# An attention and mixer block on one core: a modulation vector in the prologue, a rebuilt start of the tail, regrouped mixer channels, and hints on all final branches

## The chip, the core and the metric

The kernel runs on one core of one Trainium2 chip. The metric is the device time of one execution in microseconds (us), and each kernel was run several times. "Span" is the part of that time which the profiler's trace covers; 4 to 6 us of each execution lie outside it. Five engines matter here: TensorE (PE in the profile, its weight loads PEld), VectorE (DVE), ScalarE (ACT), GpSimd (POOL) and SyncE (SP), which in this kernel does nothing but issue DMA transfers.

## The reference, cut to what matters

```python
mod = (silu(c) @ w_mod).reshape(1, 6, 1, 640)       # sa, ca, ga, sb, cb, gb: vectors 0 to 5
h = layernorm(x) * (1 + ca) + sa                    # x: 2048 x 640
x = x + ga * attention(h, k_cache, v_cache, wq, wo) # 32 heads of 128, 2048 keys
h = layernorm(x) * (1 + cb) + sb
x = x + gb * B(h)

def B(x):                                           # the mixer and an MLP
    h = gelu(layernorm(x) @ w1)                     # 640 channels in 4 groups of 160
    hs = concat(shift(h[group], by +1, -1, +2, -2 rows)) @ w2
    x1 = x + hs
    return x1 + gelu(layernorm(x1) @ w3) @ w4       # 1728 wide
```

## The kernel before: the parts that the change and the argument touch

The kernel records every operation with a planned duration and a priority, and a scheduler written in Python sets the order of each engine before the program is built. The 2048 queries are four chunks of 512 (`NC`), and the 32 heads are eight groups of four. A *step* is one head on one chunk. It has eight score pairs of two 128x512 matmuls each, and one exponential of 128x1024 per pair. So there are 128 steps and 1024 exponentials.

```python
MS = 17
for n, p in enumerate((2, 4, 3, 5)):            # four modulation vectors, in steps 17 to 24
    dma("SP", ... w_half[n % 2], w_mod[:, p * D:(p + 1) * D] ...)                 # 800 KB each
    for hf in range(2):
        for k in range(KT):                     # five 128x320 matmuls per half
            P.op("PE", ... matmul(m, s_bc[:, k, :], w_half[n % 2][:, k, sl]) ...)

def load_head(h):                               # heads 1 to 4 in the prologue, the others later
    load_k(h, pr, need=from_slot(n))            # four DMA transposes
    load_v(h, pr + 1, need=from_slot(n + 1))    # 512 KB

# ... cut: ln1, q_proj, step, wo_group ...
def mlp_in(ch, prio):                           # the mixer's input: two layernorms of one chunk
    tail = ch == NC - 1
    eng = "DVE" if tail else "POOL"             # chunks 0 to 2: GpSimd; ACT for the roots
    # ... cut ...

TAIL = ("A0 WO B0 B1 B2 A1 B3 A2 ...").split()  # A: mixer in, WO: last projection, B: mixer out, C, D: MLP
# ... cut ...
for (p0, p1, dl) in segs[n]:                    # 128 channels cross a group's edge: 9 GELUs per chunk
    P.op("ACT", ... activation(us_ap[p0:p1, n, ch * QC + 2 + dl: ...], m[p0:p1, :], GELU) ...)

# ... cut: the last instruction on each engine jumps over a general fallback
br = eng.br_cmp(redo[e], 0, comp_op="IS_EQ", on_true="done", on_false="general")
if eng is nc.tensor:
    br.branch_hint(hint["PE"])
```

## Time and profile before

| | before |
|---|---|
| time, median of 3 | 1400.83 us (1400.35 to 1401.30) |
| span of the profiled run | 1394.5 us |
| PE busy | 1367.3 us, 98% |
| first score matmul of the attention | 16.54 us |
| end of the last exponential | 1204.95 us |
| from there to the end of the span | 189.5 us |

Next, the stretches of the kernel before in which the change works: busy us of each engine (with counts), the mean granted PE clock, the busy share of the DMA engines and GB/s.

```profile
core 0: us, PE busy (x) PEld busy (x) DVE busy (x) ACT busy (x) POOL busy (x), PEclk, DMA share, GB/s
...
40.00:50.00 10.00, 9.89 (x108) 7.13 (x109) 4.20 (x11) 9.44 (x11) 0.00 (x0) 1.00 0.69 189
...
1200.00:1210.00 10.00, 9.54 (x86) 6.03 (x86) 6.63 (x19) 8.88 (x14) 7.96 (x9) 1.00 0.59 186
1210.00:1220.00 10.00, 6.32 (x31) 3.43 (x30) 3.43 (x8) 8.33 (x12) 4.77 (x4) 0.83 0.53 94
1220.00:1230.00 10.00, 9.13 (x56) 5.36 (x56) 9.51 (x25) 6.27 (x11) 1.74 (x2) 1.00 0.18 35
```

PE has a hole in 1210 to 1220, where the clock is also below 1: the clock record has it at half from 1215.66 on, for 3.41 us. These are its waits in the tail (who waited for whom, us in total, times, longest), and ScalarE's table loads there:

```profile
PE f_S L668 <- ACT f_PQ L836: 3.3, 1, 3.3
PE f_S L850 <- ACT f_PQ L836: 0.8, 1, 0.8
PE f_S L832 <- ACT f_PQ L836: 0.8, 1, 0.8
```

```profile
L836 ACT ACT_TABLE_LOAD x3 | 3.8, 1283 | 1.1 <-POOL f_PQ L825 1.1
...
L477 ACT ACT_TABLE_LOAD x2 | 2.6, 1283 | 0.0
L478 ACT ACT_TABLE_LOAD x2 | 2.6, 1283 | 0.0
```

L836 is the mixer's GELU, L477 and L478 the logarithm and exponential for the reciprocal roots. PE waits for ScalarE, and ScalarE spends 9 us of some 20 on seven table loads. A load costs its own 1.28 us and little more here: one starts at 1207.92 us, as the GELU before it ends, and the next operation starts at 1209.22, 1.30 us later.

### The profile page before, as it was taken

What the parts mean: (1) busy time and instruction counts of PE and PEld (TensorE: products, weight loads), DVE (VectorE), ACT (ScalarE), POOL (GpSimd) and SP (SyncE); (2) the same over time, 40 slices, a digit from 0 to 9 for tenths busy, and PEclk for the clock granted to TensorE, in tenths of its full rate; (3) what the DMA queues carried; (4) which work ended last, traced back from release to release, by engine and by line L of the source; (5) the groups of instructions that cost most, each with busy time, mean ns of one, the idle gap of its engine ahead of it and who ended that gap; (6) DMA issues with size and microseconds to landing.
All of it is one profiled execution on the core that took longest, in us unless ns stands there. A gap on an engine that the chain in (4) does not pass through costs nothing.

```text
span 1394.5 us, 29726 instructions
## 1 busy us (share of the span) xinstructions
PE 1367.3 (98%) x12941; PEld 943.8 (68%) x13176; DVE 518.6 (37%) x1337; ACT 1125.9 (81%) x1195; POOL 123.8 (9%) x106
## 2 busy tenths in 40 slices
PE   8999999999999999999999999999999999899998
PEld 6667776776777777777776777777777666555554
DVE  5453323233323332233323332333223345585552
ACT  5988888888888889888888888888988888864222
POOL 0000000000000000000000000001233376600000
PEclk9999999999999999999999999999999999999999
DMA  9652623261215221241115112612353112411210
GB/s 204 128 107 38 136 57 86 49 107 35 47 35 88 54 47 35 58 84 39 43 24 99 32 39 31 107 35 47 54 107 98 17 36 51 111 39 48 34 39 24
DMA packets 258963, 88.82 MB, mean 64 GB/s; under 512 B 236625, under 2 KB 257554, under 8 KB 258834
## 3 DMA queue, kind: packets, MB, share of 16 engines
q1 hardware_dynamic: 256210, 85.41, 30.9%
q8 instruction: 104, 1.70, 0.5%
q10 hardware_dynamic: 2624, 1.51, 0.5%
q14 instruction: 25, 0.20, 0.1%
HBM read 43.48 MB, written 2.62 MB: 33 GB/s over the span
## 4 chain that ended last, share of the span: by engine, by line
PE 96%; ACT 2%; issue 1%; DVE 0%; DMA 0%; POOL 0%; ACTq 0%; POOLq 0%
PE f_O L731 34%; PE f_S L712 29%; PE f_M L643 10%; PE f_M L668 10%; PE f_S L890 2%; PE f_M L890 2%; PE f_S L877 2%; PE f_O L877 2%; ACT f_PQ L714 1%; PE f_S L850 1%; PE f_M L850 1%; PE f_S L413 1%; PE f_S L832 1%; ACT f_PQ L836 1%; PE f_O L832 0%
## 5 line engine op out<-in xcount | busy, mean ns | idle before, releaser
L714 ACT ACTIVATE f_PQ<-f_S 128x1024 bf16<-128x1024 f32 x1024 | 1041.5, 1024 | 143.5 <-PE f_S L712 106.4
L731 PEld LDWEIGHTS f_O<-f_KV,f_PQ 128*128 128x128 bf16 x8192 | 593.7, 98 | 231.9 <-ACT f_PQ L714 0.5
L731 PE MATMUL f_O<-f_KV,f_PQ 128*128 128x129 bf16 x8192 | 720.2, 220 | 7.8 <-ACT f_PQ L714 0.3
L712 PE MATMUL f_S<-f_PQ,f_KV 128*128 128x512 bf16 x1856 | 671.3, 379 | 5.3 <-ACT f_PQ L714 2.2
L676 DVE TENSOR_TENSOR f_y<-f_M,f_y 128x320 f32<-128x320 f32 x192 | 94.4, 492 | 524.1 <-PE f_M L668 524.1
L668 PE MATMUL f_M<-f_wo,f_OO 128*128 128x320 bf16 x992 | 270.2, 299 | 0.0
L712 PEld LDWEIGHTS f_S<-f_PQ,f_KV 128*128 128x128 bf16 x2048 | 196.2, 97 | 34.4 <-ACT f_PQ L714 3.9
L643 PE MATMUL f_M<-f_hT,f_wq 128*128 128x512 bf16 x608 | 170.8, 379 | 2.2 <-DVE f_hT L557 0.5
L511 POOL TENSOR_TENSOR f_y<-f_y,f_mod 128x640 f32<-128x640 f32 x40 | 61.4, 1542 | 1056.9 <-DVE f_y L676 1049.5
L668 PEld LDWEIGHTS f_M<-f_wo,f_OO 128*128 128x128 bf16 x992 | 95.1, 98 | 27.9
L740 DVE TENSOR_TENSOR f_OO<-f_O,f_rl 128x256 bf16<-128x256 f32 x256 | 108.4, 423 | 8.3
L646 DVE CAST f_PQ<-f_M 128x512 bf16<-128x512 f32 x128 | 88.5, 691 | 54.3 <-PE f_M L643 53.7
L643 PEld LDWEIGHTS f_M<-f_hT,f_wq 128*128 128x128 bf16 x640 | 62.3, 98 | 62.9 <-DVE f_hT L557 1.0
L738 DVE RECIPROCAL f_rl<-f_O 128x2 f32<-128x2 f32 x256 | 43.5, 170 | 47.2 <-PE f_O L731 42.9
L880 ACT ACTIVATE f_OO<-f_O 128x512 bf16<-128x512 f32 (+1 forms) x28 | 16.7, 596 | 36.2 <-PE f_O L877 36.1
L674 DVE COPY f_y<-f_M 128x320 f32<-128x320 f32 x32 | 15.7, 490 | 67.4 <-PE f_M L668 67.4
L880 ACT ACTIVATE f_OO<-f_S 128x512 bf16<-128x512 f32 (+1 forms) x28 | 16.7, 596 | 27.5 <-PE f_S L877 27.5
L890 PE MATMUL f_S<-f_KV,f_OO 128*128 128x320 bf16 x224 | 34.3, 300 | 0.0
L890 PE MATMUL f_M<-f_KV,f_OO 128*128 128x320 bf16 x224 | 34.3, 300 | 0.0
L472 DVE BATCH_NORM_STATS2 f_small<-f_y 128x6 f32<-128x320 f32 x64 | 29.3, 478 | 7.9 <-POOL f_y L511 7.9
L890 PEld LDWEIGHTS f_M<-f_KV,f_OO 128*128 128x128 bf16 x224 | 20.6, 97 | 14.0 <-issue 5.5
L890 PEld LDWEIGHTS f_S<-f_KV,f_OO 128*128 128x128 bf16 x224 | 20.5, 97 | 13.3 <-issue 4.2
(119 smaller groups left out, 517.4 us busy)
## 6 DMA issues: line engine op xcount, KB each, us to landing
f_KV<-in_A_v_cache_dram SPq DMA_DIRECT2D x31, 512.0 KB, 4.9
f_wo<-in_A_wo_dram SPq DMA_DIRECT2D x8, 640.0 KB, 4.3
f_xin<-in_A_x_dram SPq DMA_DIRECT2D x15, 320.0 KB, 3.8
f_wq<-in_A_wq_dram SPq DMA_DIRECT2D x7, 640.0 KB, 4.5
f_W<-in_w_mod_dram SPq DMA_DIRECT2D x4, 800.0 KB, 4.8
out_dram<-f_xin SPq DMA_DIRECT2D x16, 160.0 KB, 1.8
f_KV<-in_B_w_dram SPq DMA_DIRECT2D x5, 432.0 KB, 3.5
f_KV<-in_A_k_cache_dram SPq DMA_TRANSPOSE x128, 2.8
```

The source lines that it names most:

```text
L511: P.op(eng, lambda e: e.tensor_tensor(out=out, in0=a, in1=b, op=op), COST[eng][0], rd, wr, prio, lat=300 if eng == "POOL" else None)
L643: P.op("PE", lambda e, i=i, kk=kk: e.matmul(m.ap, wq_t[g % 2][:, kk, hh * 128:(hh + 1) * 128], hT_t[ch][:, kk, :], start=(i == 0), stop=(i ...
L646: P.op("DVE", lambda e: e.tensor_copy(q.ap, m.ap), 690, (m,), (q,), s * NP - 90)
L668: P.op("PE", lambda e, m=m, qt=qt, hf=hf, hh=hh: e.matmul(m[:, 0:HD], OT_ap[gs][:, qt, hh, :], wo_t[g % 2][:, hh, hf * HD:(hf + 1) * HD], ...
L676: P.op("DVE", lambda e, m=m, yt=yt: e.tensor_tensor(out=yt.ap, in0=m[:, 0:HD], in1=yt.ap, op=ALU.add), 490, (m, yt), (yt,), s * NP - 60)
L712: P.op("PE", lambda e, sp=sp, r=r, kt=kt: e.matmul(sp[:, r * QC:(r + 1) * QC], K_ap[b][:, kt * 128:(kt + 1) * 128], q.ap, start=True, stop ...
L714: x = P.op("ACT", lambda e, sp=sp, pt=pt: e.activation(pt.ap.rearrange("p k q -> p (k q)"), sp.ap, ACT.Exp, scale=SCALE), 1021, (sp,), (pt ...
L731: ins = e.matmul(o[bk][:, w * 129:w * 129 + 129], pt[:, r, qt * 128:(qt + 1) * 128], V_ap[b][:, u, 0:129], start=(u == 0 and w == 0), stop ...
L738: P.op("DVE", lambda e, ov=ov, i0=i0: e.reciprocal(rl_t[:, i0:i0 + 2].unsqueeze(2), ov[:, 0:258].rearrange("p (u d) -> p u d", u=2)[:, :, ...
L740: evac.append(P.op("DVE", lambda e, ov=ov, i0=i0, bk=bk: e.tensor_tensor(out=On_ap[gs][:, 2 * bk:2 * bk + 2, hh, :], in0=ov[:, 0:258].rear ...
L877: P.op("PE", lambda e, m=m, f=f, kk=kk, fs=fs: e.matmul(m[0:fs, :], w3_ap[:, kk, f * 128:f * 128 + fs], nT_ap[ch][:, kk, :], start=(kk == ...
L890: P.op("PE", lambda e, f=f, hf=hf, fs=fs: e.matmul(m[:, hf * 512:hf * 512 + HD], gT_ap[0:fs, f, i * 128:(i + 1) * 128], w4_ap[f][0:fs, hf ...
```

## The change

The intent was to take work out of the PE-bound part and to close the hole at the start of the tail:

1. Modulation vector 2 (ten matmuls) moves from steps 17 and 18 into gaps of the prologue. Its 800 KB are loaded at the very start, and several other early loads get a *gate*, a dependency on an earlier weight load, so that they don't compete with it.
2. The prologue loses 48 filler matmuls and VectorE loses a cast.
3. The projection of the last group of heads is spread anew.
4. At the start of the tail, half of chunk 2's mixer input goes to VectorE, with a Newton root instead of ScalarE's tables (chunk 3's had such a root before), and chunk 2's last additions go there from GpSimd. For chunk 3, most of the scaling that ScalarE did goes to VectorE too. The mixer's channels are regrouped so that a chunk has five GELUs instead of nine, and other work stands between A0 and WO.
5. The last tile is stored in two halves.
6. The final branch of each engine is hinted, not PE's alone.

Core of the diff:

```diff
-    P.op("DVE", lambda e: e.tensor_copy(s_bc.ap, ...), 800, (c_f,), (s_bc,), 0.5)
+    P.op("POOL", lambda e: e.tensor_copy(s_bc.ap, ...), 1000, (c_f,), (s_bc,), -290, lat=300)
-    spin(12, -281)                                   # and 36 more fillers further down
-    load_k(0, -296)
-    load_v(0, -290, "ACT", gate=(wm[3],))
+    load_k(0, -296, gate=(wm[2],))                   # all of K0's transposes but the first
+    dma("ACT", lambda e: e.dma_start(pre_ap, mod_src(2)), 800, (wm[1],), pre_t, -292)
+    for hf in range(2):
+        modulation(2, hf, pre_ap, pre_t, "O%d" % hf, lambda k, hf=hf: (-262, 0.5)[hf] + 0.01 * k, -50)
+    load_v(0, -290, "ACT", gate=(wm[1],))
-        load_k(h, pr, need=from_slot(n))
-        load_v(h, pr + 1, need=from_slot(n + 1))
+        load_k(h, pr, (wm[2],) if h == 1 else (), from_slot(n))
+        load_v(h, pr + 1, gate=(wm[2],) if h == 1 else (), need=from_slot(n + 1))
-    for n, p in enumerate((2, 4, 3, 5)):
+    for n, p in enumerate((4, 3, 5)):
-            rstd_act(g, a, a + 2, prio - 100)        # ln1 of a chunk: slack tells the scheduler to plan later
+            rstd_act(g, a, a + 2, prio - 100, 0.0 if ch == 0 else 1500.0)
...
-        eng = "DVE" if tail else "POOL"
+            pool = ch < NC - 2 or (ch == NC - 2 and a == 0)
+            # not pool: scalar_tensor_tensor on DVE, twice per tile, and rstd_dve (Newton, 128x2 operations)
-    TAIL = ("A0 WO B0 B1 B2 A1 B3 A2 B4 ...
+    TAIL = ("A0 B0 B1 B2 A1 B3 WO B4 B5 A2 ...
...
-            if eng is nc.tensor:
-                br.branch_hint(hint["PE"])
+            eng.br_cmp(...).branch_hint(hint[name])  # on all five engines
```

## The prediction

> **What bounds it now.** First part of the page: PE busy 1367.3 of 1394.5 us (98%); the chain of waits is 96% PE. Taking matmul starts from the timeline [...], PE loses about 4.4 us in each 100 us between 200 and 1100 us, in gaps of 0.22 us that no wait explains. The change leaves this and the matmuls alone. What can be won lies where PE waits more: the first 17 us (first score matmul at 16.54), 1200 to 1240 (windows view: PE busy 34.1 of 40 us, 9.1 us of loss where 1.8 is normal) and the last 4.5 us after PE's last matmul (1389.9). About 6 us of the 1400.8 lie outside the span.
>
> **What changes, and its worth.**
> 1. Ten 128x320 matmuls (modulation vector 2; 136 ns apart in the chain) leave the PE-bound stream. Five go behind the first Q projection, where before filler matmuls ran while PE waited for the eviction (0.69 us), five behind the first score pair, where PE waited for ACT. Gain 1.3 us, if their 800 KB are there: before, 512 KB issued at 7.7 landed at 14.7.
> 2. Prologue: VectorE loses a 0.80 us cast (to GpSimd) ahead of the normalisation, two transposes go ahead of the last mod column, 48 filler matmuls go. First score matmul about 1.2 us earlier, at 15.3. The extra load delays V, wq and K1 some 3 us; they had 2 to 5 us of room: I take off 0.5.
> 3. Attention, last group: output projection spread anew; 1100 to 1200 lost 5.3 us against 4.4 normal. Gain 0.5.
> 4. Tail start. The timeline shows seven table loads of 1.28 us from 1206 to 1225[...], with PE idle 3.4 us before the chunk 3 projection at 1214.3, then 0.6, 1.0 and 1.0 us. The change leaves four loads, cuts mixer GELUs from 9 per chunk to 5 (0.60 us each, whatever their partitions), puts half of chunk 2's norm on VectorE, and puts B0 to B2 and A1 between A0 and the projection. PE then has about 8 us of work while ACT loads tables for 4.5 us. Of 7.3 us I expect 5.5 back; VectorE (18.5 of 20 us busy in 1240 to 1260) gets more work.
> 5. Last tile in halves: the final two 0.82 us operations become two of 0.49. Gain 0.7.
> 6. Hints on all five final branches. [...]PE alone is hinted now. This falls after the span; no trace shows it. Guess: 1 us, range 0 to 2.
>
> **Sum:** 1.3 + 0.7 + 0.5 + 5.5 + 0.7 + 1.0 = 9.7 us. Predicted 1391 us, 8 in 10 within 1386.5 to 1395.5. Faster by over 2% (below 1373) 1%, within 2% 98%, slower 1%.
>
> **What would show it.** First score matmul near 15.3; PE busy of 1200 to 1240 near 38; four table loads in the tail; PE's last matmul near 1381; time less span down from 6 to 5. Steady loss unchanged.
>
> **What would make it wrong.** The modulation weights or V landing late, stalling PE in the first steps; Ln and Exp on ACT waiting for VectorE's statistics and holding the second chunk's GELUs; VectorE late with accumulator evictions, so PE waits for banks between 1220 and 1290[...].

For term 6, its 1.0 us is a bare guess of mine; e15 below measures it. The 4.4 us of loss in each 100 us are what matmuls started later than their columns account for; in the trace, matmuls of 512 columns usually start 0.216 us apart. The 1.28 us of a table load are in the trace of the kernel before (1283 ns each).

## More of the kernel before

SyncE issues nearly all loads, in one order. K comes through DMA transposes, four per head, and V as one plain load of 512 KB. Beyond the first chunk the normalised queries (hT) are transposed by DMA too.

From the page of the kernel before: first the busy time of each engine with its number of instructions, then two of the costliest groups (line, engine, operation, output and input, shapes, count, busy us, mean ns of one, idle time before).

```profile
PE 1367.3 (98%) x12941; PEld 943.8 (68%) x13176; DVE 518.6 (37%) x1337; ACT 1125.9 (81%) x1195; POOL 123.8 (9%) x106
...
L712 PE MATMUL f_S<-f_PQ,f_KV 128*128 128x512 bf16 x1856 | 671.3, 379 | 5.3 <-ACT f_PQ L714 2.2
...
L712 PEld LDWEIGHTS f_S<-f_PQ,f_KV 128*128 128x128 bf16 x2048 | 196.2, 97 | 34.4 <-ACT f_PQ L714 3.9
```

PE bounds the kernel. But compare the counts: the program loads weights once for each matmul, 13176 times, and the trace holds only 12941 matmuls. In L712 alone there are 1856 records for 2048 matmuls.

Last, SyncE's queue near the start of the kernel before (start, duration, issues merged in order). It pauses for no more than 0.12 us here, and one DMA transpose mostly takes 1.27 us of it:

```profile
26.42 6.12 SPq L562 DMA_TRANSPOSE f_hT<-f_xn  x4
32.58 0.58 SPq L577 DMA_DIRECT2D f_KV<-in_A_v_cache_dram  x1
33.21 6.08 SPq L572 DMA_TRANSPOSE f_KV<-in_A_k_cache_dram  x4
39.41 0.51 SPq L577 DMA_DIRECT2D f_KV<-in_A_v_cache_dram  x1
```

The last line is the V of the fourth head, V3 from here on. It landed at 43.98 us.

## The result, and the profile after

| | before | after |
|---|---|---|
| time, median of 4 of the same rounds | 1400.59 us (1399.84 to 1401.30) | 1399.88 us (1398.47 to 1400.74) |
| ratio, 95% interval | | 0.9994 [0.9977, 1.0011] |
| span of the profiled run | 1394.5 us | 1395.5 us |
| first exponential starts | 17.19 us | 16.05 us |
| end of the last exponential | 1204.95 us | 1207.40 us |
| from there to the end of the span | 189.5 us | 188.1 us |

A ratio is the mean time of one kernel's runs over that of the other's in the same rounds, so it is not quite the ratio of the medians in the table. The class is "same", as I had given 98%; but it would have been so for the forecast gain too, since the class changes at 2%. I had said 1391 within 1386.5 to 1395.5. Of the 9 us, 0.7 came between the medians, and that is not clear of noise.

The kernel after, the same lines of its page (the score matmuls are L724 now):

```profile
PE 1380.0 (99%) x13128; PEld 941.8 (67%) x13128; DVE 540.2 (39%) x1380; ACT 1107.2 (79%) x1164; POOL 110.4 (8%) x96
...
L724 PE MATMUL f_S<-f_PQ,f_KV 128*128 128x512 bf16 x2048 | 727.6, 379 | 0.6 <-ACT f_PQ L726 0.5
...
L724 PEld LDWEIGHTS f_S<-f_PQ,f_KV 128*128 128x128 bf16 x2048 | 196.8, 98 | 31.1 <-ACT f_PQ L726 1.4
```

This trace happens to be complete: 13128 matmuls for 13128 weight loads. Here PE loses only about 0.2 us per 100 us in the steady part, counting what a matmul starts later than the usual spacing (216 ns for 512 columns, 136 for 320). The "4.4 us in each 100 us" of the prediction was 224 missing records of 512 columns (192 in L712, 32 in L643) at 0.216 us each, 48 us in all. There is next to no steady loss. And the 13 us by which PE's busy time seems to have grown are records that the first trace lacked. A trace of the kernel before that was taken later, in experiment e5, holds all 13176.

Stretches of the kernel after:

```profile
core 0: us, PE busy (x) PEld busy (x) DVE busy (x) ACT busy (x) POOL busy (x), PEclk, DMA share, GB/s
...
40.00:50.00 10.00, 7.19 (x71) 4.44 (x69) 3.40 (x10) 6.29 (x8) 0.00 (x0) 0.99 0.82 184
...
1200.00:1210.00 10.00, 9.53 (x98) 6.17 (x94) 9.62 (x15) 9.26 (x13) 7.83 (x8) 1.00 0.44 125
1210.00:1220.00 10.00, 5.97 (x23) 2.38 (x22) 7.91 (x31) 2.83 (x5) 0.00 (x0) 0.83 0.27 54
1220.00:1230.00 10.00, 9.72 (x58) 5.36 (x56) 8.32 (x26) 7.43 (x12) 1.73 (x2) 1.00 0.48 131
```

There is a new hole in 40 to 50 us. The hole in 1210 to 1220 is as large as it was, but ScalarE is no longer the busy engine beside it: VectorE is. PE's waits of the kernel after, first in 38 to 52 us, then in the tail:

```profile
PE f_O L743 <- DMA f_KV<-in_A_v_cache_dram: 2.6, 1, 2.6
...
PE f_O L854 <- DVE f_OO L752: 3.8, 1, 3.8
PE f_O L681 <- DVE f_tmp L692: 0.4, 1, 0.4
```

ScalarE's table loads in the same stretch are four instead of seven:

```profile
L857 ACT ACT_TABLE_LOAD x2 | 2.6, 1283 | 0.0
L480 ACT ACT_TABLE_LOAD x1 | 1.3, 1283 | 0.0
L481 ACT ACT_TABLE_LOAD x1 | 1.3, 1283 | 0.0
```

And the kernel after's SyncE queue, to be read against the one above:

```profile
30.47 4.68 SPq L574 DMA_TRANSPOSE f_KV<-in_A_k_cache_dram  x2
35.19 2.60 SPq L564 DMA_TRANSPOSE f_hT<-f_xn  x2
37.84 1.26 SPq L574 DMA_TRANSPOSE f_KV<-in_A_k_cache_dram  x1
39.14 2.60 SPq L564 DMA_TRANSPOSE f_hT<-f_xn  x2
41.78 1.26 SPq L574 DMA_TRANSPOSE f_KV<-in_A_k_cache_dram  x1
43.08 0.78 SPq L579 DMA_DIRECT2D f_KV<-in_A_v_cache_dram  x1
```

V3 is issued at 43.08 instead of 39.41 and lands at 48.37 instead of 43.98, while PE came for it at about 45.9.

**Where the span went.** Following the exponentials through both traces gives this sum (after minus before):

| stretch | predicted | in the traces |
|---|---|---|
| to the first exponential | -1.2 | -1.14 |
| from there to step 22, with the wait at 48.5 | +0.5 | +4.59 |
| modulation, exponentials 176 to 240 (ten matmuls fewer) | -1.3 | -1.36 |
| from there to the last exponential (last group) | -0.5 | +0.35 |
| last exponential to PE's last matmul (tail) | -5.5 | -0.88 |
| PE's last matmul to the end | -0.7 | -0.54 |
| sum, span | -8.7 | +1.02 |
| time less span, these two runs | -1.0 | -0.7 |

Two terms failed: what the start gives back, and the tail. The experiments are about these two, and about the hints.

Both waits do more harm than they last. Near the end of each (from 49.72 and from 1213.66 us), the clock record shows a stretch of 3.413 us at 0.5, as it did once in the tail of the kernel before (from 1215.66). The 512-column matmuls that follow the wait in the tail are 0.43 us apart in it instead of 0.22. By these figures each stretch costs up to 1.7 us more (an estimate: half of 3.413).

Where a wait falls may matter, and not only how long it is. In these two traces the half-clock stretches start whole multiples of 3.413 us apart (341.00 in the kernel after, 52.00 in the kernel before, where the second starts after PE's last matmul). So I cut both traces into windows of 3.413 us, counted from their first stretch. In the window just before a stretch PE was busy for 0.36 and 0.00 of the time in the kernel after and for 0.28 in the kernel before, or, where PE had finished, for 0.10 and 0.06. In every other one of some 400 windows of each trace it was busy for at least 0.64. PE's busy time is modelled and the trace of the kernel before lacks records, so these shares are rough. That more than these two traces would look the same is not shown. The wait for V3 fell mostly into one window (0.36 busy). In e13, below, with the tail of the kernel after, no stretch came there: its granted clock of 0.997 over the span leaves no room for one beside the 6.8 us at half clock in its start (an estimate: the span can have lost at most 0.0035 of 1396.6 us, 4.9 us, of which the start takes 3.4, and another stretch would take 1.7). So whether a wait of this length brings one is in part luck of the run.

### The profile page after: what moved, and what is told of

It reads as the page before. It is cut to its first block, busy times and chain, and to the rows that moved or that the text cites. A ratio compares the mean times of both kernels' runs of the same rounds, so it can differ in the third digit from the quotient of the medians.

```text
span 1395.5 us, 29875 instructions
## 1 busy us (share of the span) xinstructions
PE 1380.0 (99%) x13128; PEld 941.8 (67%) x13128; DVE 540.2 (39%) x1380; ACT 1107.2 (79%) x1164; POOL 110.4 (8%) x96
## 4 chain that ended last, share of the span: by engine, by line
PE 96%; DVE 1%; DMA 1%; SPq 1%; issue 0%; ACT 0%
PE f_O L743 33%; PE f_S L724 31%; PE f_M L656 10%; PE f_M L681 10%; PE f_M L918 3%; PE f_O L904 2%; PE f_S L904 2%; PE f_S L918 2%; PE f_S L877 1%; PE f_O L854 1%; PE f_S L854 1%; PE f_M L877 1%; DMA f_wq<-in_A_wq_dram 1%; DMA f_W<-in_w_mod_dram 0%; DMA f_KV<-in_A_v_cache_dram 0%; PE f_M L601 0%
## 5 line engine op out<-in xcount | busy, mean ns | idle before, releaser
L724 PE MATMUL f_S<-f_PQ,f_KV 128*128 128x512 bf16 x2048 | 727.6, 379 | 0.6 <-ACT f_PQ L726 0.5
L724 PEld LDWEIGHTS f_S<-f_PQ,f_KV 128*128 128x128 bf16 x2048 | 196.8, 98 | 31.1 <-ACT f_PQ L726 1.4
L656 PE MATMUL f_M<-f_hT,f_wq 128*128 128x512 bf16 x640 | 176.3, 379 | 1.8 <-DMA f_wq<-in_A_wq_dram 0.7
L514 POOL TENSOR_TENSOR f_y<-f_y,f_mod 128x640 f32<-128x640 f32 x36 | 55.6, 1559 | 820.0 <-DVE f_y L689 819.9
L752 DVE TENSOR_TENSOR f_OO<-f_O,f_rl 128x256 bf16<-128x256 f32 x256 | 108.4, 423 | 8.2
L907 ACT ACTIVATE f_OO<-f_S 128x512 bf16<-128x512 f32 x28 | 16.7, 597 | 38.9 <-PE f_S L904 38.9
L918 PE MATMUL f_M<-f_KV,f_OO 128*128 128x320 bf16 x252 | 38.6, 300 | 0.0
L520 ACT ACTIVATE f_xn<-f_y,f_small 128x640 bf16<-128x640 f32 x10 | 9.1, 915 | 30.4 <-DVE f_small L499 25.6
L918 PE MATMUL f_S<-f_KV,f_OO 128*128 128x320 bf16 x196 | 30.0, 300 | 0.0
```

What stands on the lines that cost most here:

```text
L514: P.op(eng, lambda e: e.tensor_tensor(out=out, in0=a, in1=b, op=op), COST[eng][0], rd, wr, prio, lat=300 if eng == "POOL" else None)
L656: P.op("PE", lambda e, i=i, kk=kk: e.matmul(m.ap, wq_t[g % 2][:, kk, hh * 128:(hh + 1) * 128], hT_t[ch][:, kk, :], start=(i == 0), stop=(i ...
L724: P.op("PE", lambda e, sp=sp, r=r, kt=kt: e.matmul(sp[:, r * QC:(r + 1) * QC], K_ap[b][:, kt * 128:(kt + 1) * 128], q.ap, start=True, stop ...
L752: evac.append(P.op("DVE", lambda e, ov=ov, i0=i0, bk=bk: e.tensor_tensor(out=On_ap[gs][:, 2 * bk:2 * bk + 2, hh, :], in0=ov[:, 0:258].rear ...
L918: P.op("PE", lambda e, f=f, hf=hf, fs=fs: e.matmul(m[:, hf * 512:hf * 512 + HD], gT_ap[0:fs, f, i * 128:(i + 1) * 128], w4_ap[f][0:fs, hf ...
```

## The experiments

All but e5 are edits of the kernel after. All gave correct results. The table has what was measured; "spans" are the means over the timed runs. For the 41 timed runs of the kernel before that ran beside the experiments, the span was 1394.9 on average (1394.1 to 1397.6). "33rd" is the start of the 33rd exponential, the first after step 3, against that of the kernel before; "tail" is from the end of the last exponential to the end of the span (before: 189.5). Both are from one profiled run each. The profiled run need not be a typical one, and one kernel's runs differ by up to 8 us (e7). The kernel after, e3, e4, e7 and e15 all have the same start, and their 33rd lies anywhere from +3.09 to +7.86: a difference of 2 or 3 us in this column is no evidence by itself. In the lists of clock and span of every run, the long runs are those with the lower mean clock: e7's had 0.997 with 1398.6 us and 1.000 with 1390.8. That clock is worth some 4 us of e7's 7.8 (an estimate: 0.003 of the span), so about half of the scatter goes with the lower clock. Waits in the text are those of the waits view. The recorded texts count them from one matmul's start to the next, less the usual spacing (0.216 us for 512 columns), which gives some 0.16 us more (2.7 for 2.6 us, 3.9 for 3.7 or 3.8).

| | time, median (range) | ratio to before | mean span | 33rd | tail |
|---|---|---|---|---|---|
| after | 1399.88 (1398.47 to 1400.74) | 0.9994 [0.9977, 1.0011] | 1394.7 | +3.70 | 188.1 |
| e1 | 1403.64 (1400.64 to 1405.06) | 1.0012 [0.9994, 1.0030] | 1398.5 | +6.71 | 189.2 |
| e2 | 1398.45 (1397.26 to 1400.99) | 0.9979 [0.9963, 0.9996] | 1393.8 | +2.43 | 188.2 |
| e3 | 1399.90 (1398.81 to 1401.20) | 0.9990 [0.9974, 1.0007] | 1395.4 | +5.52 | 187.1 |
| e4 | 1398.66 (1397.26 to 1400.58) | 0.9984 [0.9966, 1.0002] | 1393.7 | +3.09 | 187.5 |
| e5 | 1399.02 (1397.99 to 1399.07) | 0.9987 [0.9970, 1.0004] | 1393.2 | -0.78 | 189.5 |
| e6 | 1399.35 (1397.01 to 1402.11) | 0.9994 [0.9977, 1.0011] | 1394.9 | +1.37 | 189.3 |
| e7 | 1398.12 (1395.55 to 1403.58) | 0.9977 [0.9960, 0.9993] | 1394.2 | +7.86 | 186.8 |
| e8 | 1397.68 (1397.28 to 1399.22) | 0.9979 [0.9962, 0.9995] | 1393.1 | +3.33 | 187.5 |
| e9 | 1397.61 (1396.76 to 1398.94) | 0.9983 [0.9968, 0.9999] | 1393.3 | -1.15 | 188.2 |
| e10 | 1401.90 (1400.75 to 1403.67) | 1.0014 [0.9999, 1.0030] | 1397.3 | +3.36 | 188.5 |
| e11 | 1399.41 (1397.74 to 1400.14) | 0.9990 [0.9975, 1.0006] | 1394.7 | +1.98 | 188.2 |
| e12 | 1400.14 (1397.94 to 1402.76) | 0.9997 [0.9983, 1.0011] | 1395.2 | +1.31 | 190.0 |
| e13 | 1399.54 (1397.65 to 1402.67) | 0.9993 [0.9979, 1.0007] | 1394.9 | +5.95 | 186.9 |
| e14 | 1400.76 (1399.16 to 1402.24) | 0.9999 [0.9983, 1.0014] | 1396.1 | +5.07 | 188.3 |
| e15 | 1401.71 (1399.18 to 1404.35) | 1.0003 [0.9990, 1.0017] | 1396.4 | +7.13 | 188.2 |
| e16 | 1396.82 (1394.29 to 1400.00) | 0.9975 [0.9961, 0.9988] | 1392.0 | +4.29 | 185.9 |
| e17 | 1399.54 (1396.83 to 1402.61) | 0.9985 [0.9972, 0.9999] | 1394.4 | +5.10 | 188.5 |
| e18 | 1397.59 (1395.46 to 1399.11) | 0.9977 [0.9963, 0.9991] | 1392.8 | +4.49 | 185.8 |

### e1, e2, e5, e6: which part of the start is to blame?

The gates idle SyncE's queue for 2.6 us at 5.7 us, the early 800 KB take DMA time, and the 1.5 us of planning slack on the first layernorm's root changes the order in SyncE's queue. Each was undone alone, and the slack was also added alone to the kernel before.

```diff
 e1, the gates go
-    load_k(0, -296, gate=(wm[2],))
+    load_k(0, -296)                      # likewise for wq, K1 and V1
 e2, vector 2 back in the steady part, gates kept
-    for n, p in enumerate((4, 3, 5)):
+    for n, p in enumerate((2, 4, 3, 5)): # and the early load and its two modulation() calls removed
 e5, in the kernel before
-            rstd_act(g, a, a + 2, prio - 100)
+            rstd_act(g, a, a + 2, prio - 100, 0.0 if ch == 0 else 1500.0)
 e6, in the kernel after: the reverse of e5
```

> The changed kernel with the new gates taken off (the K, V and wq loads that wait for the third slab of modulation weights wait for it no longer); the early modulation vector and its 800 KB stay. Theory G (the gate idles the SP queue 2.6 us and the transposes behind it, each 1.27 us of queue time, stay late by that): V of the fourth head lands at 45.8 us or sooner instead of 48.4, PE's wait for it is under 0.5 us instead of 2.6, no half-clock stretch near 50 us, and the 33rd exponential starts about 1 us before that of the kernel before instead of 3.7 us after it; time 1395 to 1396. Rival M (the 800 KB moved into the start hold up everything behind them): V still lands near 48, wait 2 us or more, time near 1400.

> The changed kernel with the modulation vector 2 back in the steady part (its load and ten matmuls as before the change); the gates stay. Theory G (gate): the wait for V of the fourth head stays at 2 us or more, and the time is 1 us longer than that of the changed kernel, as the ten matmuls come back. Rival M (the 800 KB): the wait is gone, the 33rd exponential starts about 1 us before that of the kernel before, and the time is 1396 to 1397 although ten matmuls came back.

> The kernel before with one argument of the change alone: the reciprocal deviation of the chunks 1 to 3 of the first norm is planned 1.5 us later. Theory S (this planning slack puts the small ACT operations later in ACT's order, and so splits the four transposes of chunk 1's hT between those of the fourth head's K on the SP queue, so that K and V of that head land late): the SP order is now V, two hT, two K, two hT, two K, V; V of the fourth head is issued 2 us or more later than the 39.4 of the kernel before and lands after 46; PE waits 1 to 3 us for it near 46 to 49, with a half-clock stretch behind, and the 33rd exponential starts 2 to 5 us later than in the kernel before; time 1403 to 1405. Rival N (it needs the changed start, its gates or its 800 KB): no wait over 0.5 us there, time within 1 us of the kernel before.

> The changed kernel with that planning slack taken back to zero, gates and early 800 KB kept. Theory S: hT is transposed earlier, V of the fourth head lands at 46 or sooner, PE waits under 1 us, no half-clock stretch near 50, the 33rd exponential starts 0 to 1 us before that of the kernel before; time 1395 to 1396. Rival N (start as a whole is late by the 800 KB and the gates together): the wait stays over 2 us, time near 1400.

Without the gates V3 was issued at 39.71, as early as before, and landed at 45.42; but then an hT transpose landed at 47.26, PE waited 4.6 us for it, and a half-clock stretch of 6.8 us followed. In median time and mean span e1 is more than 3 us slower than the kernel after. So the gates alone are not the cause. Without the early load (e2) V3 still landed at 47.08, and PE waited 2.8 us. So the load alone is not the cause either. The slack alone, in the kernel before (e5), put the hT transposes between those of K, as the kernel after has them in a somewhat other order, and brought no wait over 0.7 us. Taking it away from the kernel after (e6) left a wait of 2.8 us. The slack alone is not the cause. (e5's mean span is even 1.7 us under that of the kernel before, though the interval of its time still includes 1.)

### e9, e10, e11: load and gates one by one, on the same footing

With the slack at 0 in all of them, these three and e6 make a two by two table.

```diff
 e9:  e1 + e2 + e6 (neither load nor gates)
 e10: e1 + e6 (load, no gates)
 e11: e2 + e6 (gates, no load)
```

> The changed kernel with all three changes of its start's loads undone at once: no early modulation load, no gates, no planning slack; the shorter prologue and everything later as changed. Neither the load alone, nor the gates with the slack, nor the slack alone have explained the wait for the fourth head, so the theory now is Q: the SP queue and the DMA engines are full for the first 45 us, the kernel before had about 2 us of room there, and each of load and gates takes more than that. Q expects here: V or hT for the fourth step in time, wait under 0.5 us, no half-clock stretch before 1200, the 33rd exponential 0.5 to 2 us before that of the kernel before, time 1397 to 1398. Rival R (the shorter prologue itself, which asks for everything 1 to 2 us sooner, runs into the wait): the wait stays over 1 us with nothing of the load changes left.

> Of the three changes of the start's loads only the early modulation load. Q expects a wait of 2 to 5 us in the fourth step (for V or for hT, whichever stands last on the SP queue), 33rd exponential 1 to 6 us later than in the kernel before. If the load is harmless alone: no wait over 0.5 us and the 33rd exponential 1 us or more ahead.

> Of the three changes of the start's loads only the gates. Q expects the queue 1 to 2 us behind the kernel before, V of the fourth head landing 45 to 46, and a wait of 0 to 2 us, smaller than with the load. If the gates are what counts: wait of 2.5 us or more.

Mean spans (e6 is of an earlier round than the other three):

| | no early load | early load |
|---|---|---|
| no gates | 1393.3 (e9) | 1397.3 (e10) |
| gates | 1394.7 (e11) | 1394.9 (e6) |

The load by itself costs 4.0 us net. The runs of e9 (1392.5 to 1393.8) and e10 (1396.2 to 1398.5) do not overlap, so this is clear of noise. The gates by themselves cost 1.4, and with the gates the load costs only 0.2 more, as the gates were meant to bring about; but each mean is of four runs, those of e6 lie between 1392.5 and 1397.7, and these two figures could be off by 1 us. The variants without the load have the ten modulation matmuls in the steady part, which is 1.36 us of their span. So at the start the load alone costs some 5.3 us (4.0 + 1.36), and load and gates together some 2.9 (1394.9 - 1393.3 + 1.36), of which 1.36 come back later.

In single profiles the two look alike: PE waited 3.2 us for hT in e10 and 3.1 us for V3 in e11, which by my own sign for e11 (2.5 or more) would have made the gates the cause. The mean spans tell them apart, one wait does not.

e9 shows that even this is not all. It has nothing but the shorter prologue. Its 25th exponential starts 3.27 us earlier than before, but its 33rd only 1.15. PE ran ahead, and then waited 2.0 us for V3, which landed at 45.16, 1.2 later than before. PE could not use all of its head start, since the data came no earlier. This was the rival that I had left out of the prediction altogether.

### e13, e14: V3 out of the queue, or earlier in it

If the trouble is V3's place behind the transposes, moving it should end the wait.

```diff
 e13
-        load_v(h, pr + 1, gate=...)
+        load_v(h, pr + 1, "ACT" if h == 3 else "SP", gate=...)
 e14
+        load_v(h, pr + (0.005 if h == 3 else 1), gate=...)     # right behind its head's first K transpose
```

> The changed kernel, with only the load of the fourth head's V (512 KB) moved from SyncE's queue, where it stood 18th behind the transposes and was issued at 43.1 us, to ScalarE's queue behind the 12th exponential, about 29 us. Theory Q (the load is late because of its place in SyncE's in-order queue): V lands before 42 us, the 2.7 us wait at 48.5 and the half-clock stretch after it go, the 33rd exponential stands within 1.5 us of before's (it stood 3.7 later), and the time falls by 3 to 5 us to about 1396. Rival D (the DMA engines are full until 48 us): V may land early, but then the second head's V or the transposes of hT land as much later, and PE waits over 2 us for one of those before 52 us; time 1399 to 1401.

> The changed kernel, with the same load kept on SyncE's queue but put right behind the first K transpose of its head: issue at about 35 instead of 43 us. Theory Q: V lands about 41 us, the hT transposes and the last K transpose each come 0.7 us later, no wait over 1 us in step 3, time near 1396. Rival D: the wait moves to hT, which then lands after 46 us, wait of 2 to 4 us, time 1399 to 1401. If e13 is free of the wait and e14 is not, it is the queue's length, not the DMA engines.

Both failed, and in the way that rival D had named. In e13 V3 was issued at 29.16 and landed at 35.35, ten microseconds before it was needed. But PE now waited 3.7 us for the last hT transpose. The wait of e13 in 38 to 52 us, and its SyncE queue, in which the K transposes behind V2 and V3 are held for 5.33 and 1.26 us instead of 3.38 and 1.26:

```profile
PE f_M L656 <- DVE f_hT L566: 3.7, 1, 3.7
```

```profile
30.38 6.63 SPq L574 DMA_TRANSPOSE f_KV<-in_A_k_cache_dram  x2
37.05 2.60 SPq L564 DMA_TRANSPOSE f_hT<-f_xn  x2
39.68 1.26 SPq L574 DMA_TRANSPOSE f_KV<-in_A_k_cache_dram  x1
40.99 2.60 SPq L564 DMA_TRANSPOSE f_hT<-f_xn  x2
```

The releaser named is VectorE, which works on hT after it has been transposed; but VectorE was idle then, and the last transpose was issued at 42.31 and landed at 47.50. It is a DMA wait. In e14 the same transpose landed at 47.19. What is loaded up to there is the same in the kernel after, e1, e13 and e14, and whatever is put first, the later one of V3 and the last hT landed between 47.2 and 48.4.

### e17: is it the instruction fetch?

The last transpose of e13 took 5.2 us to land, its two neighbours 2.65. The DMA view of e13 for 42.3 to 47.5 us shows what else was under way, by queue and kind:

```profile
q1 hardware_dynamic: 1880, 0.46, 85.7%
q14 instruction: 2, 0.02, 3.7%
q8 instruction: 1, 0.02, 1.1%
```

There is one packet of 16 KB of kind "instruction", at 44.49 us, and two of 8 KB, at 44.86 and 44.89. The 16 KB ones come once per about 250 PE instructions, so I take them for PE's program: the kernel after has 105 such packets for 13128 matmuls and as many weight loads. They are not harmless to others. Take the DMA transposes of the kernel after between 100 and 1150 us that had no plain load beside them. The 103 in which no such packet started between issue and landing took 2.52 us to land (median), and the 23 in which one did took 3.97. In the kernel before it was 2.53 (89) and 3.97 (27).

To test it, the fetch was moved. The 80 filler matmuls at the start became 21 wider ones, as long in sum, so that PE's program has 118 instructions fewer before any given point.

```diff
 e17 = e13 and:
-        P.op("PE", lambda e: dummy(e, n), n * 56, ...)             # n matmuls of 128 columns
+        P.op("PE", lambda e: broad(e, (n + 2) // 4), n * 56, ...)  # a quarter as many of 512
```

> e13 (the fourth head's V on ScalarE's queue) with the 80 warm-up filler matmuls of 128 columns at PE's start made 21 of 512 columns: as much PE time, but 59 matmuls and 59 weight loads fewer, so that PE comes to each later 16 KB of its instruction stream about 118 instructions later. The fourth large instruction fetch, at 44.5 us in e13 and in the middle of the last hT transpose, then falls at 49 us or later. Theory I (the instruction fetch holds the transpose in flight by about 2.5 us): the last hT transpose lands within 3 us of its issue, about 45; PE's wait falls from 3.9 to under 1.5 us, no half-clock stretch before 60 us, 33rd exponential from 5.95 later than before's to within 2.5, time about 1395.5. Rival D (DMA data, fetch harmless): hT lands after 46.5, wait over 2.5 us with a half-clock stretch, time as e13's, 1399.5.

The fetch moved as planned, from 44.5 to 54.8 us. The wait fell from 3.7 to 2.8 us, and the stretch at half clock from 6.8 to 3.4, but theory I had asked for less than 1.5 and no stretch. (The kernel after and e15, with the same start, differ by as much: 2.6 us and 3.4 against 3.5 and 6.8.) The fetch before it had moved as well, to 39.4 us, where two other hT transposes then took 4.3 and 3.5 us to land and SyncE's queue waited with them; and the two small fetches still fell into the last one (3.9 us). So transposes with a fetch in flight land later: that is shown by the medians. But in a stretch where transposes follow each other without pause, moving one fetch only moved the delay. Theory I fell as the explanation of the wait.

### e3, e4, e7: the tail's new wait

The trace of the kernel after names the wait at 1214.0: 3.8 us for L752, VectorE's eviction of the last attention output. VectorE was behind by then, busy for 9.42 us of 1190 to 1200 and 9.62 of 1200 to 1210. The kernel before had 5.08 and 6.63. Part of that was not planned. Groups of the kernel after on VectorE in 1198 to 1214 us:

```profile
L791 DVE SCALAR_TENSOR_TENSOR f_y<-f_y,f_small,f_mod 128x640 f32<-128x640 f32 x2 | 2.9, 1498 | 0.0
...
L493 DVE SCALAR_TENSOR_TENSOR f_small<-f_small 128x2 f32<-128x2 f32 x3 | 2.2, 730 | 0.1
...
L495 DVE SCALAR_TENSOR_TENSOR f_small<-f_small 128x2 f32<-128x2 f32 x3 | 2.0, 656 | 0.0
L494 DVE TENSOR_TENSOR f_small<-f_small 128x2 f32<-128x2 f32 x3 | 1.8, 612 | 0.1
```

An operation on 128x2 elements that averages 0.7 us, with single ones up to 1.48, isn't working that long. GpSimd's operations on 128x640 ran beside it, about 1.5 us each. In the trace the three longest (1.47 to 1.48 us) each end within 0.03 us of the end of a GpSimd operation that had started 0.1 us earlier; once GpSimd is done, at 1212.7 to 1213.5 us, the same three take 0.14 to 0.16 us. The operations that got longer here, the new Newton steps and normalisations, have two inputs in SBUF. Theory P in the recorded texts is that GpSimd's work holds them up. Against their durations in e4, below, the eight of them that ran beside GpSimd lasted some 6.3 us longer in sum (an estimate). The kernel before had one such case there (L915, 0.74 us), and I could have seen it. Its neighbours L913 and L914 have one input and ran beside the same GpSimd operation without loss:

```profile
L915 DVE TENSOR_TENSOR f_flb<-f_small 128x1 bf16<-128x1 f32 x1 | 0.7, 739 | 0.0
...
L913 DVE TENSOR_SCALAR f_small<-f_small 128x1 f32<-128x1 f32 x1 | 0.2, 154 | 0.0
L914 DVE TENSOR_SCALAR f_small<-f_small 128x1 f32<-128x1 f32 x1 | 0.2, 153 | 0.0
```

e3 orders the late work of chunk 2 behind the evictions. e4 gives the other half of chunk 2 to VectorE too, so that GpSimd is idle there. e7 gives that half back to GpSimd.

```diff
 e3: VectorE's share of chunk 2 is ordered after the last two evictions
+            late = () if pool or tail else tuple(evac[-2:])
 e4
-            pool = ch < NC - 2 or (ch == NC - 2 and a == 0)
+            pool = ch < NC - 2
 e7
+            pool = ch < NC - 1
```

> The changed kernel with VectorE's share of chunk 2's norm ordered behind the eviction of the last attention output; nothing else. Theory P (VectorE[...] comes late to that eviction, and PE waits for the bank): PE's wait before the third group of the first mixer projection goes from 3.8 us to under 0.5, the half-clock stretch at 1214 is gone, the span from the last exponential's end to the end goes from 188 to about 183 us, time about 5 us less than the changed kernel's: 1394 to 1395. The two-input operations of VectorE that run beside GpSimd's still last 1.4 to 1.5 us. Rival T (the table loads and GELUs of ACT bound this stage whatever VectorE does): the wait moves to a bank that ACT reads, and the time stays within 1.5 us of the changed kernel's.

> The changed kernel with both halves of chunk 2's norm on VectorE, so that GpSimd has nothing to do at the end of the attention; nothing else. Theory P[...]: the 128x2 Newton steps (SCALAR_TENSOR_TENSOR and TENSOR_TENSOR on two SBUF inputs) last 0.15 us everywhere between 1200 and 1215 us instead of 1.47, the 128x640 ones 0.85 instead of 1.3 to 1.5, the PE wait for the last eviction is under 1 us, time 1394 to 1397. Rival D (VectorE is slow by its own chain of short dependent steps): they stay at about 1.5 us, VectorE has more of them, and the PE wait grows beyond 3.8 us.

> The changed kernel with the second half of chunk 2's norm back on GpSimd; all else as changed. Theory P (what costs is VectorE's new share[...]): the wait for the last eviction (3.8 us) is gone and nothing over 1 us takes its place; the stretch from the last exponential's end to the end of the span falls from 188.1 to 183 to 185; but seven table loads return. Rival T (the seven table loads were the cause of the wait in the kernel before, and the new order alone does not hide them): the stretch stays at 187 or more, with PE waiting for ACT.

In e3 the wait for L752 went, and 2.7 us came back at 1232.6, where WO's matmuls waited for the postponed root (L495): the stall had moved. In e4 the same three operations, on VectorE in the same window:

```profile
L495 DVE SCALAR_TENSOR_TENSOR f_small<-f_small 128x2 f32<-128x2 f32 x6 | 0.9, 157 | 0.0
L494 DVE TENSOR_TENSOR f_small<-f_small 128x2 f32<-128x2 f32 x6 | 0.8, 153 | 0.0
L493 DVE SCALAR_TENSOR_TENSOR f_small<-f_small 128x2 f32<-128x2 f32 x6 | 0.8, 146 | 0.0
```

With GpSimd idle, each takes 0.15 us, twice as many in less than half the time. That settles that GpSimd's work beside them made them long; by what mechanism is not shown. But the tail of e4 is 187.5 us, 0.6 better than the kernel after, no more. VectorE has more to do now and is busy for 9.2 us of 1200 to 1210, and PE waits 1.8 us for VectorE's copies of the mixer's rest channels (L860) and 1.5 in WO, for an eviction and a root. In e7 the half-clock stretch in the tail is gone (granted clock 1.00 throughout 1190 to 1260), and six smaller waits (0.3 to 1.4 us) stand in place of the one. The best tail of the three is e7's, 186.8; the best mean span, e4's, is 1 us under the kernel after's. But these tails are not on the same footing: the kernel after and e4 have a half-clock stretch in theirs (granted clock 0.83 in 1210 to 1220) and e7 has none. e13, with the tail of the kernel after, happened to have none either and took 186.9, and e16, with e4's tail and no stretch (granted clock 1.00 in 1200 to 1240), took 185.9; e18, with the same tail, took 185.8. So e7's edit is worth nothing that shows, and e4's about 0.6 to 1.1 us, with the stretch or without.

### e8, e12, e16, e18: combinations

```diff
 e8  = e4 + e6
 e12 = e9 + e7, and higher priority for VectorE's evictions of WO (WOD -200 to -1500) and its mixer copies
 e16 = e4 + e13
 e18 = e4 + e17
```

> Slack at zero and both halves of chunk 2's norm on VectorE: one table load in the tail. If theories S and P hold and add up: 33rd exponential 0 to 1 us ahead of the kernel before, stretch from the last exponential's end to the end about 187.5 as measured with this norm alone, time 1394 to 1395. If S falls, 1398 to 1399.

> Plain start as in the first of these runs, chunk 2's norm all on GpSimd, and VectorE's evictions of the chunk 3 projection and the four small shifts of the mixer ahead of its norm work. Theory P for the tail (VectorE comes late to what PE waits for): from the last exponential's end to the end of the span 184 to 186 us, no half-clock stretch; with the plain start a time of 1394 to 1396, better than both kernels. If the order on VectorE does not matter: 187 or more, time 1397 to 1398.

> e13's edit and e4's (both halves of chunk 2's normalisation on VectorE) together. Theory Q for the start[...]: neither the wait at 48.5 nor the 3.9 us wait at 1214, 33rd exponential within 1.5 us of before's, last exponential to span end about 187.5, time about 1395 and the interval wholly under 1.0. If e13's gain fails to come, it is e4's time, 1398.7.

> e17 with e4's tail (both halves of chunk 2's normalisation on VectorE). Theory I[...]: start as in e17, last exponential to span end 186 to 187.5 as in e4 and e16, time 1392 to 1394.5, faster than both kernels with the interval under 1.0. If theory I is wrong, e16's time, 1396.8.

e12 was meant as the mended version and failed: its tail is 190.0, the worst of all. With the evictions first, the second normalisation of the mixer came too late, and PE waited twice for its transposed input:

```profile
PE f_S L899 <- DMA f_wq<-f_xn: 2.7, 1, 2.7
PE f_O L849 <- DMA f_wq<-f_xn: 2.4, 1, 2.4
```

e16 is the quickest kernel: 1396.82 us, ratio 0.9975 with the whole interval under 1. Its start is no better than the kernel after's (33rd +4.29, a wait of 3.6 us). It gains in the tail, 185.9, where no half-clock stretch came. I had expected 1395 and a start without the wait. It is not clear of e7, e8 and e18, whose ratios are 0.9977 and 0.9979. e18 with the fetch moved is no better (1397.59), as e17 would have it. e8 agrees with e4. Putting both halves of chunk 2 on VectorE was worth 0.9 us of mean span (e4 against the kernel after), 1.8 (e8 against e6), 3.0 (e16 against e13) and 1.7 (e18 against e17).

### e15: the hints

```diff
-            eng.br_cmp(...).branch_hint(hint[name])        # on all five
+            br = eng.br_cmp(...)
+            if eng is nc.tensor:
+                br.branch_hint(hint["PE"])
```

> The changed kernel with the branch hint on PE alone, as before the change. If the hints on the other four engines are worth what I guessed, time minus span of its runs goes from about 5.0 back to about 5.8 us and the time rises by 0.5 to 1 us against the changed kernel's 1399.9 (so 1400.4 to 1401); if they are worth nothing, time minus span stays at 4 to 5.5 and the time is that of the changed kernel. The span is the same either way, within the scatter of its start.

Time less span was 5.20 us on average in e15 (4.78 to 5.47, 5 runs), 5.10 in the kernel after (4.54 to 5.47, 4 runs), 4.82 over all kernels with five hints (73 runs, 3.89 to 5.84), and 5.59 in the kernel before (41 runs). So the hints are worth 0.1 us by the direct pair and 0.4 by the pool, and another 0.4 that I had put down to them is there without them. The higher time of e15 itself is in its span, from a start that fell badly (33rd +7.13); it says nothing about the hints. Smaller than guessed is shown; the exact size is open.

## Why the prediction was wrong, point by point

**What bounds the kernel: right, with a wrong number.** PE bounds it. "PE loses about 4.4 us in each 100 us" was an artefact of missing matmul records. It entered no term of the sum, but with it I set 1.8 of the 9.1 us lost in 1200 to 1240 aside as normal. The complete trace of e5 has some 8.3 us of loss there by the same count, and next to none of it is normal. So the 7.3 us that I called winnable came near by luck: the missing records had made both figures too large.

**Term 1, the ten modulation matmuls: right.** Predicted 1.3, measured 1.36.

**Term 2, the prologue: the gain was right, the step "they had 2 to 5 us of room: I take off 0.5" failed.** The first exponential came 1.14 earlier (predicted 1.2), and then 4.59 were lost instead of 0.5. I had judged the room of V, wq and K1 by their own need, one by one. But SyncE's queue runs almost without pause to about 46 us, and when a load went round it, its transposes were slower (e13: two held it for 5.33 and 1.26 us instead of 3.38 and 1.26); so a delay at its head comes out at its end, where V3 and the last hT transpose had no room. I listed the modulation weights or V landing late as what would make the prediction wrong, and gave it too little weight. What the runs put in place of the step: the early load without the gates costs 4.0 us net of the 1.36 it gives back (5.3 at the start); load and gates together cost some 1.5 net (2.9 at the start); and the shorter prologue alone loses about 2 of its 3.3 us to the same limit. Moving the late piece (e1, e13, e14) only changed which piece was late. That nothing but less data or more time would help is argued from this, not shown: no variant with less to load before 47 us than e9 was run.

**Term 3, the last group: wrong by a little.** Predicted 0.5 gained; 0.35 was lost. The cause stays open: no experiment was spent on it.

**Term 4, the start of the tail: this step failed most.** I wrote "Of 7.3 us I expect 5.5 back"; 0.88 came. The table loads went from seven to four as predicted, and ScalarE, the engine that PE had waited for, was no longer late. But I added up what the change takes from ScalarE and GpSimd and didn't do the sum for VectorE in 1190 to 1210, which went from 11.7 to 19.0 us of 20. Part of that (the two-input operations beside GpSimd, 0.15 to 1.48 us) was unplanned, and e4 shows it; part was the planned work, and the two other orders that were tried (e3, e12) and the half given back to GpSimd (e7) gained 1.3 us of tail at most. That no other order would do is not shown. The wait went from ScalarE to VectorE. My warning, "VectorE late with accumulator evictions", named the mechanism, though it put the place at 1220 to 1290. And I had looked for VectorE's load 40 us too late, in 1240 to 1260.

**Term 5, the last tile: right.** Predicted 0.7; 0.54.

**Term 6, the hints: right in sign, too large.** Guessed 1.0, for a reason that no trace shows; e15 leaves 0.1 to 0.4.

The signs I had named did tell the terms apart. The first score matmul came at 15.41 (15.3 predicted) and the table loads were four, as said; but PE's busy time in 1200 to 1240 rose only from 34.1 to 34.8 instead of to 38, and its last matmul ended at 1391.5 instead of 1381.

## What to carry to other kernels

When a queue or an engine has no pause, a change in front of it has to be costed at its end: ask for the last piece in the queue, not for the room of the pieces that were moved. When work is moved from the engine that others wait for, do the busy sum of the receiving engine in the stretch just before the wait, with the durations that its operations have next to their new neighbours. And before trusting a loss that is spread evenly over a trace, compare the number of records with the number that the program issues.
